# Attention with two mixture layers on one core: weight halves issued by ScalarE, a new order in the numerators, other banks for one slot sum

## Chip, cores and metric

One core of one Trainium2 chip runs the whole program. The metric is device time in microseconds, the median of three runs of the kernel.

## What is computed

A linear attention (features `exp(proj)` and `exp(-proj)`) feeds a soft mixture of 8 experts through 32 slots, and that feeds a second, dense mixture of 8 experts. Cut to what matters:

```python
# q, k, v: 4 batches x 8 heads x 576 x 64; w_phi 64 x 128
def phi(x):
    proj = einsum('bhsd,df->bhsf', x, w_phi)
    proj = proj - max(abs(proj), axis=-1, keepdims=True)
    return concatenate([exp(proj), exp(-proj)], axis=-1)
q_p, k_p = phi(q), phi(k)
kv  = einsum('bhsf,bhsd->bhfd', k_p, v);  z = sum(k_p, axis=2)
num = einsum('bhsf,bhfd->bhsd', q_p, kv)
den = einsum('bhsf,bhf->bhs', q_p, z) + 1e-06
x   = num / den                                   # 2304 tokens x 512

logits = x @ phi                                  # first mixture: 8 experts, 4 slots each
d = softmax of logits over the tokens;  slot_input = d.T @ x
slot_out[e] = relu(slot_input[e] @ w1[e]) @ w2[e] # w1 512 x 1024, w2 1024 x 512
x = softmax of logits over the slots @ slot_out

# second mixture: gates P by 8 rounds of row and column normalising, then for each expert
out += P[:, e] * (relu(x @ w1[e]) @ w2[e])
```

## The kernel before

The 2304 tokens are 18 tiles of 128. One hand-ordered loop, `for i in range(NT + LAG + 1)` (L414), carries the attention. Iteration `i` works on key tile `i` and, seven iterations late (`LAG = 7`), on query tile `t = i - 7`. So iterations 0 to 6 do keys alone, 7 to 16 do keys and queries, and from 17 on (`alone(i)`, L203) no new key tile is projected; those are called lone iterations here. All engines but GpSimd issue in the order in which the program is written (class `InOrder`, L43, with helper line L51, which is why nearly all rows of the trace carry L51).

What an iteration does, in order. SyncE issues the load of key tile `i + 3`, of a value block for tile `i + 2`, and of query tile `t + 3`, 256 KB each. TensorE projects the next query tile (`pq`, 32 matmuls) and the next key tile (`pk`), turns the finished rows of tile `t - 1` (`xt`), and turns query tile `t` in two halves (`ut`, `q_transpose(t, 0)` and `q_transpose(t, 1)`). ScalarE takes from each `ut` tile two exponentials (`phiq`, first of plus, then of minus). TensorE then does the logits (`lg`), adds the key tile into the sums (`kvacc`, 64 matmuls), and `q_num` multiplies the two query halves with the finished sums (`num`, 32 matmuls each). ScalarE takes four exponentials for the next key tile (`phik`) ahead of the numerators. In `q_num` the loop over the 4 heads is outside and the loop over the two signs `c` is inside it.

PSUM has named banks for this. `halves(t, hh)` (L206) gives banks A and E in the iterations with keys and E and C in lone ones, and both the `ut` tile and the `num` tile of a half are taken from that same bank: `num` can be written when both exponentials have read `ut`. Query projections use A and B.

Between the iterations a generator, `slot_inputs(g)` (L273), advances for each group of four tiles: a maximum, its broadcast, exponentials `dd`, and then the sums `pcs` (with ones) and `psi` (with the x tiles), which VectorE adds into `cs` and `si`. In group 1 `psi` lies in bank B and `pcs` in C, in groups 2 to 4 in A and B. Group 1's sums fall into the first lone iteration, number 17.

The weights of the first mixture come in 32 units of 1 MB, `units[u]`, each [128, 2048]; 22 of them are loaded during the attention. Units 0 to 3 (pool `wa`) and 8 to 14 (`early`, `wb`) are loaded in iterations 9 to 19 (`early_units`, L395) as two halves of 512 KB by `load_half` (L81), which issues on SyncE's queue: the first half between the key load and the value load, the second after the query load. Units 15 to 21 follow in iterations 18 to 24, both halves at the iteration's end (L487), in pool `wk`, which is opened where the key tiles lay, in iteration 18. Unit 4 waits for the last `pq` (its memory held the query tiles), units 5 to 7 for the end of the last numerators. After the loop the slots' experts run from about 193 us (`ph`, `po`), and then the second mixture, which is by far the longest stage.

Of the kernel before, what the change touches and what calls it, by code (L numbers as in the profile page):

```python
# [14 lines left out]
B, H, S, D = 4, 8, 576, 64  # L15
F = 128
NTOK, DM = B * S, H * D
NT = NTOK // 128
# [36 lines left out]
def tile_kernel(ctx: ExitStack, tc: tile.TileContext, a):  # L55
    nc = tc.nc
    PE, V, A, G, SP = nc.tensor, nc.vector, nc.scalar, nc.gpsimd, nc.sync

    const = ctx.enter_context(tc.tile_pool(name="const", bufs=1, side="left"))
    wa = ctx.enter_context(tc.tile_pool(name="wa", bufs=4, side="left"))  # L60
    early_cm = tc.tile_pool(name="early", bufs=1, side="left")
    early = early_cm.__enter__()
# [11 lines left out]
    unit_t = {}  # L74
# [6 lines left out]
    def load_half(pool, u, h):  # L81
        name, e, n = units[u]
        if h == 0:
            unit_t[units[u]] = pool.tile([128, 2048], F32, tag="w", name=f"{name}_{e}_{n}")
        r = slice(h * 1024, (h + 1) * 1024)
        SP.dma_start(out=unit_t[units[u]][:, r], in_=a[name][e, :, n * 2048:(n + 1) * 2048][:, r])

    def w1_unit(name, e, n):
        return unit_t[name, e, n].rearrange("p (k f) -> p k f", k=2)
# [16 lines left out]
    def mm(name, bank=None):  # L106
        if bank is None:
            bank = "ABCDE"[turn_of[0] % 5]
            turn_of[0] += 1
        return pmm.tile([128, 512], F32, tag=bank, name=name)  # L110
# [53 lines left out]
    def k_exp(t):  # L164
        us = uk_t.pop(t)
        phik = kp.tile([128, H, 2, F], F32, tag="phik", name=f"phik{t}")
        for j in range(2):
            for c in range(2):
                A.activation(out=phik[:, j::2, c, :], in_=h4(us[j]), func=AF.Exp, scale=1.0 if c == 0 else -1.0)
        phik_t[t] = phik  # L170
# [32 lines left out]
    def alone(i):  # L203
        return i + 1 >= NT
# [4 lines left out]
    def q_transpose(t, hh):  # L209
        ps = mm(f"ut{t}_{hh}", halves(t, hh))  # L210
        for j in range(4):
            PE.transpose(ps[:, j * 128:(j + 1) * 128], uq_t[t][hh][:, j * 128:(j + 1) * 128], ident)
        phiq = qp.tile([128, 2, 512], F32, tag="phiq", name=f"phiq{t}_{hh}", bufs=3)
        for c in range(2):
            A.activation(out=phiq[:, c], in_=ps, func=AF.Exp, scale=1.0 if c == 0 else -1.0)
        phiq_t[t, hh] = phiq
        if hh:
            uq_t.pop(t)
# [7 lines left out]
    def q_num(t, hh):  # L226
        if hh == 0:
            x_t[t] = (const if (t + 2) % XR < 6 else qp).tile([128, DM], F32, tag=f"x{(t + 2) % XR}", name=f"x{t}", bufs=1)
        phiq = phiq_t.pop((t, hh))
        ps = mm(f"num{t}_{hh}", halves(t, hh))  # L230
        for j in range(4):
            for c in range(2):
                for g in range(2):
                    b = (128 * t + 64 * g) // S
                    PE.matmul(
                        ps[g * 64:(g + 1) * 64, j * XW:(j + 1) * XW],
                        phiq[:, c, j * 128 + g * 64:j * 128 + (g + 1) * 64],
                        kvs_t[b][:, hh, j, c, :],
                        start=c == 0, stop=c == 1,
                    )  # L240
        pv = ps[:, 0:4 * XW].rearrange("p (h w) -> p h w", h=4)
        rd = qp.tile([128, 4, 1], F32, tag="rd", name=f"rd{t}_{hh}", bufs=2)
        V.tensor_scalar_add(rd, pv[:, :, XW - 1:XW], 1e-6)
        V.reciprocal(out=rd, in_=rd)
        V.tensor_tensor(
            out=x_t[t].rearrange("p (h d) -> p h d", h=H)[:, hh::2, :],
            in0=pv[:, :, 0:D], in1=rd.to_broadcast([128, 4, D]), op=ALU.mult,
        )
# [24 lines left out]
    def slot_inputs(g):  # L273

        ts, n = groups[g], len(groups[g])
        lgg = lg[:, ts[0]:ts[0] + n, :]
        gm4 = first.tile([128, 4, NS], F32, tag="gd", name=f"gm4{g}", bufs=1)
        if len(ts) == 2:
            V.tensor_tensor(out=gm4, in0=lgg[:, 0:1, :].to_broadcast([128, 4, NS]), in1=lgg[:, 1:2, :].to_broadcast([128, 4, NS]), op=ALU.max)
        else:  # L280
            gm = first.tile([128, 1, NS], F32, tag="gm", name=f"gm{g}", bufs=1)
            V.tensor_reduce(out=gm.rearrange("p o j -> p (o j)"), in_=lgg.rearrange("p t j -> p j t"), axis=AX.X, op=ALU.max)
            G.tensor_copy(out=gm4, in_=gm.to_broadcast([128, 4, NS]))
        yield
        last = g == len(groups) - 1
        pt = mm(f"gmt{g}", "B" if g > 1 else "C")
        keep_busy(last, 5)
        PE.transpose(pt[:, 0:128], gm4.rearrange("p g j -> p (g j)"), ident)
        mx = first.tile([128, 1], F32, tag="mx", name=f"mx{g}", bufs=2)
        V.tensor_reduce(out=mx, in_=pt[:, 0:128], axis=AX.X, op=ALU.max)  # L290
        if g:
            V.tensor_tensor(out=mx, in0=mx, in1=run["m"], op=ALU.max)
        dg = first.tile([NS, NS], F32, tag="gd", name=f"dg{g}", bufs=1)
        V.tensor_scalar_mul(dg, ident[0:NS, 0:NS], mx[0:NS])
        if g:
            al = first.tile([128, 1], F32, tag="al", name=f"al{g}", bufs=2)
            V.tensor_tensor(out=al, in0=run["m"], in1=mx, op=ALU.subtract)
            A.activation(out=al, in_=al, func=AF.Exp)
        run["m"] = mx
        yield  # L300
        pm = mm(f"gmb{g}", "B" if g > 1 else "C")
        keep_busy(last, 6)
        PE.matmul(pm[:, 0:NS], ones[0:NS, :], dg, start=True, stop=True)
        dd = first.tile([128, 4, NS], F32, tag="gd", name=f"dd{g}", bufs=1)
        V.tensor_tensor(out=dd[:, 0:n], in0=lgg, in1=pm[:, 0:NS].unsqueeze(1).to_broadcast([128, n, NS]), op=ALU.subtract)
        A.activation(out=dd[:, 0:n], in_=dd[:, 0:n], func=AF.Exp)
        if last:

            V.tensor_scalar_mul(sels[32 * n:128], sels[32 * n:128], al[32 * n:128])
        yield  # L310
        ps, pc = mm(f"psi{g}", "A" if g > 1 else "B"), mm(f"pcs{g}", "B" if g > 1 else "C")
        keep_busy(last, 4)
        for i in range(n):
            PE.matmul(pc[32 * i:32 * i + 32, 0:2], dd[:, i], ones[:, 0:2], start=True, stop=True)
        for i in range(n):
            PE.matmul(ps[32 * i:32 * i + 32, :], dd[:, i], x_t.pop(ts[i]), start=True, stop=True)
        r = slice(0, 32 * n)
        if g == 0:
            V.memset(si, 0.0)
            V.memset(cs, 0.0)  # L320
            V.tensor_copy(out=cs[r], in_=pc[r, 0:2])
            V.tensor_copy(out=si[r], in_=ps[r])
        else:
            V.scalar_tensor_tensor(out=cs[r], in0=cs[r], scalar=al[r], in1=pc[r, 0:2], op0=ALU.mult, op1=ALU.add)
            if last:

                csel = first.tile([128, NS], F32, name="csel")
                V.tensor_scalar_mul(csel, sels, cs[:, 0:1])
                pc = mm("pcsum", "D")
                PE.matmul(pc[:, 0:NS], ones, csel, start=True, stop=True)  # L330
            V.scalar_tensor_tensor(out=si[r], in0=si[r], scalar=al[r], in1=ps[r], op0=ALU.mult, op1=ALU.add)
            if last:
                V.tensor_scalar_add(rc.rearrange("p o j -> p (o j)"), pc[:, 0:NS], 1e-9)
                V.reciprocal(out=rc, in_=rc)
        if g < 3:
            yield
            slot_norm(g, 0)
            yield
            slot_norm(g, 1)
        yield  # L340
# [51 lines left out]
        for u in units[first:first + n]:  # L392
            load_unit(pool, *u)

    early_units = {9 + n: (wa, n) for n in range(4)}  # L395
    early_units |= {13 + n: (wb if n else early, 8 + n) for n in range(7)}
    si_steps = []

    def si_step():
# [14 lines left out]
    for i in range(NT + LAG + 1):  # L414
        t = i - LAG
        if i + 3 < NT:
            load_k(i + 3)
        if i in early_units:
            load_half(*early_units[i], 0)
        for n in [n for n, (u, _) in enumerate(VBLOCKS) if u == i + 2]:  # L420
            load_v(n)
        if 0 <= t + 3 < NT:
            load_q(t + 3)
        if i in early_units:
            load_half(*early_units[i], 1)
        if i == 1:
            SP.dma_start(out=sel4, in_=a["sel4"])
            SP.dma_start(out=wg, in_=a["wg"])
# [14 lines left out]
            x_turn(t - 1)  # L443
        if 0 <= t < NT:
            q_transpose(t, 0)
            q_transpose(t, 1)
        if 0 <= t - 1 < NT:
            if alone(i):
# [8 lines left out]
            k_project(i + 1)  # L457
        if i + 1 < NT:
            k_exp(i + 1)
        if not alone(i):  # L460
            si_step()
        if 0 <= t < NT:
# [17 lines left out]
            if n == len(groups[g]) - 1:  # L480
                si_steps.append(slot_inputs(g))
        si_step()
        if i == NT:
            kstack.close()
            wk_cm = tc.tile_pool(name="wk", bufs=7, side="right", reuse_waits="tile")
            wk = wk_cm.__enter__()
        if NT <= i < NT + 7:  # L487
            load_half(wk, 15 + i - NT, 0)
            load_half(wk, 15 + i - NT, 1)
    G = InOrder(tc, G)  # L490
    const.tile([128, 8], F32, name="pad", bufs=1)
    while si_steps:
# [549 lines left out]
```

## Time and profile before

| what | value |
|---|---|
| median of three runs | 1026.72 us (1024.71 to 1028.42) |
| the profiled execution | 1025.93 us |
| its span | 1024.2 us |
| granted TensorE clock, mean | 0.994 |
| TensorE matmul busy | 999.1 us, 98% |
| attention loop | until about 187 us |

The span is what the trace covers; some 1.7 us of the execution's own time lie around it. In the timeline a row gives the start, the time from the first start to the last end, engine, operation, tiles and count, and in brackets the idle time of the engine ahead of it with what ended it. "issue" stands for idle time for which the trace shows no releaser. A window gives each engine's busy time with its instruction count, then the granted clock, the busy share of the 16 DMA engines and what they moved.

### The profile page before, as it was taken

How to read it: one execution, taken by the hardware profiler on the slowest of the kernel's cores; microseconds unless marked ns; L12 is line 12 of the kernel's file. 1: busy time of each engine (PE TensorE's matmuls, PEld its weight loads, DVE VectorE, ACT ScalarE, POOL GpSimd, SP SyncE). 2: the span in 40 equal slices, each digit the busy share in tenths (PEclk: the TensorE clock that was granted, in tenths of full speed). 3: DMA queues.
4: the chain of work that ended last, by engine and by line, in shares of the span. 5: the costliest groups of instructions: out<-in, count | busy, mean ns of one | idle time of the engine just before them, and what ended most of it. 6: DMA issues, size and time to landing. Idle time of an engine off the chain costs nothing.

```text
span 1024.2 us, 27905 instructions
## 1 busy us (share of the span) xinstructions
PE 999.1 (98%) x11645; PEld 942.6 (92%) x11645; DVE 691.8 (68%) x1408; ACT 551.3 (54%) x993; POOL 594.8 (58%) x444
## 2 busy tenths in 40 slices
PE   8999899999999999999999999999999999999998
PEld 7888787538999999999999999999999999999998
DVE  5877777405788667677666676776666767767665
ACT  5564544226566666564555555555645555455452
POOL 1101000075578757777686778587857876777543
PEclk9999999999999999999999999999999999999999
DMA  6656672994000400130021003100300040000111
GB/s 205 217 155 201 211 248 83 355 409 190 1 1 2 165 2 1 49 118 1 2 97 70 2 1 124 43 2 1 130 36 2 1 165 2 1 1 24 61 43 62
DMA packets 25437, 89.23 MB, mean 87 GB/s; under 512 B 3424, under 2 KB 6240, under 8 KB 19424
## 3 DMA queue, kind: packets, MB, share of 16 engines
q1 hardware_dynamic: 25024, 86.93, 24.2%
q8 instruction: 92, 1.51, 0.6%
q0 software_dynamic: 288, 0.52, 0.2%
q14 instruction: 33, 0.27, 0.1%
HBM read 82.72 MB, written 4.72 MB: 85 GB/s over the span
## 4 chain that ended last, share of the span: by engine, by line
PE 92%; DVE 2%; DMA 2%; issue 1%; ACT 1%; POOL 0%; SPq 0%; DVEq 0%; ACTq 0%; POOLq 0%
PE x L51 38%; PE y L51 19%; PE z L51 16%; PE num L51 4%; PE kvacc L51 3%; DMA moe_w<-in_moe_w 2%; PE pq L51 2%; PE ut L51 2%; PE pk L51 2%; PE ps L51 1%; PE lg L51 1%; PE ph L51 1%; PE po L51 1%; ACT phiq L51 1%; PE xt L51 1%
## 5 line engine op out<-in xcount | busy, mean ns | idle before, releaser
L51 POOL TENSOR_TENSOR hl_s<-s,hh_s 128x512 fp32r<-128x512 f32 x287 | 366.3, 1298 | 212.1 <-ACT hh_s L51 190.5
L51 PE MATMUL x<-w_t,hh_s 128*128 128x256 f32 x1152 | 204.8, 278 | 0.0
L51 ACT ACTIVATE hh_s<-s 128x512 fp32r<-128x512 f32 x288 | 175.6, 630 | 52.1 <-DVE s L51 49.2
L51 ACT ACTIVATE r<-z 128x512 f32<-128x512 f32 x144 | 86.2, 598 | 165.6 <-PE z L51 164.8
L51 PEld LDWEIGHTS x<-w_t,hh_s 128*128 128x128 f32 x1152 | 173.5, 188 | 0.8
L51 DVE SCALAR_TENSOR_TENSOR xo<-x,P,xo 128x256 f32<-128x256 f32 x252 | 120.5, 478 | 69.9 <-PE x L51 69.9
L51 ACT ACTIVATE hh_a<-z 128x512 fp32r<-128x512 f32 x216 | 122.2, 600 | 75.8 <-DVE s L51 74.7
L51 PE MATMUL x<-w_t,hl_s 128*128 128x256 f32 x576 | 159.6, 277 | 0.0
L51 DVE SCALAR_TENSOR_TENSOR s<-z,r 128x512 f32<-128x512 f32 x144 | 98.6, 685 | 87.6 <-ACT hh_a L51 82.6
L51 DVE SCALAR_TENSOR_TENSOR hl_a<-z,hh_a 128x512 fp32r<-128x512 f32 x216 | 146.7, 679 | 0.0
L51 PEld LDWEIGHTS x<-w_t,hl_s 128*128 128x128 f32 x576 | 108.2, 188 | 0.0
L51 PE MATMUL y<-w_t,hh_s 128*128 128x256 f32 x576 | 102.9, 278 | 0.0
L51 PE MATMUL z<-w_b,hh_a 128*128 128x256 f32 x576 | 102.4, 278 | 0.0
L51 PE MATMUL x<-w_b,hh_a 128*128 128x256 f32 x576 | 102.0, 278 | 0.0
L51 PE MATMUL x<-w_t,hh_a 128*128 128x256 f32 x576 | 101.6, 276 | 0.0
L51 PE MATMUL y<-w_b,hh_s 128*128 128x256 f32 x576 | 101.5, 276 | 0.0
L51 DVE SCALAR_TENSOR_TENSOR s<-z,s 128x512 f32<-128x512 f32 x144 | 98.2, 682 | 3.7 <-POOL hl_s L51 1.4
L51 PEld LDWEIGHTS z<-w_b,hh_a 128*128 128x128 f32 x576 | 86.6, 188 | 2.9 <-issue 2.9
L51 PEld LDWEIGHTS y<-w_t,hh_s 128*128 128x128 f32 x576 | 87.4, 188 | 0.0
L51 PEld LDWEIGHTS x<-w_b,hh_a 128*128 128x128 f32 x576 | 87.2, 189 | 0.1
L51 PEld LDWEIGHTS x<-w_t,hh_a 128*128 128x128 f32 x576 | 86.7, 188 | 0.1
L51 PEld LDWEIGHTS y<-w_b,hh_s 128*128 128x128 f32 x576 | 86.7, 188 | 0.0
(167 smaller groups left out, 1991.2 us busy)
## 6 DMA issues: line engine op xcount, KB each, us to landing
moe_w<-in_moe_w SPq DMA_DIRECT2D x46, 1024.0 KB, 6.5
moe_w<-in_moe_w SPq DMA_DIRECT2D x36, 512.0 KB, 6.3
vs<-in_vb SPq DMA_DIRECT2D x20, 256.0 KB, 2.8
kt<-in_kT SPq DMA_DIRECT2D x18, 256.0 KB, 3.7
qt<-in_qT SPq DMA_DIRECT2D x18, 256.0 KB, 3.1
out<-xo SPq DMA_DIRECT2D x18, 128.0 KB, 1.7
out<-xo SPq DMA_DIRECT2D x9, 256.0 KB, 2.0
rep<-in_rep POOLq DMA_DIRECT2D x2, 256.0 KB, 3.4
```

Source lines behind the costliest of these rows:

```text
L51: return lambda *args, **kwargs: self.tc.keep_in_program_order(make(*args, **kwargs))
```

## The change

`load_half` issues on ScalarE's queue. Its calls move: in iterations 7 to 17 the halves of units 0 to 3 and 8 to 14, in 18 to 24 those of units 15 to 21. The first half is issued between the two `q_transpose` calls, that is between the exponentials of the two query halves, the second after the next key tile's exponentials. SyncE's queue no longer holds them. Pool `wk` is opened at the end of iteration 17 instead of 18. In `q_num` the loop over the sign `c` is outside and that over the heads inside, with one `start` for each half of the partitions. In group 1 `psi` moves to bank A and `pcs` to bank B.

```diff
     def load_half(pool, u, h):
-        SP.dma_start(out=unit_t[units[u]][:, r], in_=a[name][e, :, n * 2048:(n + 1) * 2048][:, r])
+        A.dma_start(out=unit_t[units[u]][:, r], in_=a[name][e, :, n * 2048:(n + 1) * 2048][:, r])
...
-        for j in range(4):
-            for c in range(2):
+        for c in range(2):
+            for j in range(4):
                 for g in range(2):
...
-                        start=c == 0, stop=c == 1,
+                        start=c == 0 and j == 0, stop=c == 1, skip_group_check=True,
...
-        ps, pc = mm(f"psi{g}", "A" if g > 1 else "B"), mm(f"pcs{g}", "B" if g > 1 else "C")
+        ps, pc = mm(f"psi{g}", "A" if g else "B"), mm(f"pcs{g}", "B" if g else "C")
...
-    early_units = {9 + n: (wa, n) for n in range(4)}
-    early_units |= {13 + n: (wb if n else early, 8 + n) for n in range(7)}
+    attn_units = {7 + n: (wa, n) for n in range(4)}
+    attn_units |= {11 + n: (wb if n else early, 8 + n) for n in range(7)}
...
-        if i in early_units:
-            load_half(*early_units[i], 0)
...
-        if i in early_units:
-            load_half(*early_units[i], 1)
...
             q_transpose(t, 0)
+            if i in attn_units:
+                load_half(*attn_units[i], 0)
             q_transpose(t, 1)
...
             k_exp(i + 1)
+        if i in attn_units:
+            load_half(*attn_units[i], 1)
...
-        if i == NT:
+        if i + 1 == NT:
             kstack.close()
...
-        if NT <= i < NT + 7:
-            load_half(wk, 15 + i - NT, 0)
-            load_half(wk, 15 + i - NT, 1)
+            attn_units |= {i + 1 + n: (wk, 15 + n) for n in range(7)}
```

## Rows read from the trace of the kernel before

**Rows 1.** The page: TensorE's instructions, and one of the DMA queues (packets, MB, share).
```profile
PE 999.1 (98%) x11645; PEld 942.6 (92%) x11645; DVE 691.8 (68%) x1408; ACT 551.3 (54%) x993; POOL 594.8 (58%) x444
...
q8 instruction: 92, 1.51, 0.6%
```
**Rows 2.** Waits of TensorE, 20 to 192 us: total us, times, longest us.
```profile
PE num L51 <- ACT phiq L51: 1.6, 5, 0.4
...
PE pcs L51 <- DVE x L51: 1.0, 1, 1.0
```
**Rows 3.** The chain that ended last, pieces in order: start us, us, what.
```profile
41.69 0.86 issue
...
52.13 1.10 issue
...
77.80 0.68 issue
...
94.24 0.71 issue
...
108.91 2.74 issue
```
**Rows 4.** Windows from the start to the first and the last of those places.
```profile
0.00:42.00 42.00, 37.08 (x977) 33.10 (x977) 29.09 (x46) 23.97 (x42) 7.75 (x28) 1.00 0.69 212
...
0.00:110.00 110.00, 99.87 (x2622) 88.08 (x2623) 80.42 (x159) 62.24 (x122) 14.31 (x49) 1.00 0.64 202
```
**Rows 5.** Windows before and behind the longest of them.
```profile
102.00:109.00 7.00, 6.77 (x178) 5.84 (x168) 6.34 (x14) 4.92 (x10) 0.67 (x2) 1.00 0.91 291
...
112.00:115.00 3.00, 3.00 (x64) 2.88 (x64) 1.25 (x4) 0.00 (x0) 0.00 (x0) 0.54 0.13 49
```
**Rows 6.** Timeline of SyncE's issues of weight halves.
```profile
55.93 1.53 SPq L51 DMA_DIRECT2D moe_w<-in_moe_w  x1
...
87.60 0.43 SPq L51 DMA_DIRECT2D moe_w<-in_moe_w  x1
...
102.55 1.66 SPq L51 DMA_DIRECT2D moe_w<-in_moe_w  x2
...
104.73 1.43 SPq L51 DMA_DIRECT2D moe_w<-in_moe_w  x2
```
**Rows 7.** Timeline of TensorE: a dense stretch, and two projections, slow and quick.
```profile
66.30 2.06 PE L51 MATMUL kvacc<-vt,phik 128*64 128x65 f32 x64
68.20 2.04 PE L51 MATMUL num<-kvs,phiq 128*64 128x65 f32 x64
...
112.50 1.98 PE L51 MATMUL pq<-wbd,qt 64*64 64x128 f32 x32
...
121.94 1.10 PE L51 MATMUL pq<-wbd,qt 64*64 64x128 f32 x32
```
**Rows 8.** Timeline of TensorE around the slot sums of groups 1 and 2.
```profile
135.36 2.04 PE L51 MATMUL num<-kvs,phiq 128*64 128x65 f32 x64
...
140.33 1.42 PE L51 MATMUL pq<-wbd,qt 64*64 64x128 f32 x32
...
163.47 2.13 PE L51 MATMUL num<-kvs,phiq 128*64 128x65 f32 x64
...
167.54 1.10 PE L51 MATMUL pq<-wbd,qt 64*64 64x128 f32 x32 [0.28 <-DVE si L51]
```
**Rows 9.** Timeline: exponentials with keys (65 us) and alone, and lone numerators.
```profile
65.25 2.06 ACT L51 ACTIVATE phiq<-ut 128x512 f32<-128x512 f32 x4
...
174.63 2.07 ACT L51 ACTIVATE phiq<-ut 128x512 f32<-128x512 f32 x4 [1.42 <-PE ut L51]
...
175.77 2.13 PE L51 MATMUL num<-kvs,phiq 128*64 128x65 f32 x64 [0.30 <-ACT phiq L51]
```
**Rows 10.** The chain in the slots' experts, and a window of that stage.
```profile
214.69 14.27 DMA moe_w<-in_moe_w
...
200.00:225.00 25.00, 24.74 (x306) 10.50 (x302) 3.13 (x18) 6.64 (x12) 14.81 (x11) 1.00 1.01 405
```

## Prediction

> **What bounds the kernel now.** I read the page first: TensorE's matmuls are busy 98% of the span [rows 1], so a change that takes no TensorE work away can win only where TensorE stands idle or runs slowly. The second mixture offers nothing of that kind and isn't touched. I therefore read TensorE's waits in the attention, then the chain that ended last in that stretch, then windows and timelines around each gap.
>
> In the attention the chain runs through TensorE nearly all the time. What it loses has three forms. The largest are five gaps that the chain calls issue, of 0.86, 1.10, 0.68, 0.71 and 2.74 us, 6.1 us together [rows 3]: nothing that the trace shows released TensorE. The second is one wait of 1.0 us of `pcs` for VectorE's `x`. The third is five short waits of `num` for the exponentials, 1.6 us in all [rows 2].
>
> What are the five gaps? The page lists 92 packets of 1.51 MB on an instruction queue, 16.4 KB each, and TensorE executes 11,645 matmuls and as many weight loads, so one packet is worth 253 of them [rows 1]. Up to the first gap the windows count 977 + 977 = 1954 of these, up to the last 2622 + 2623 = 5245: the difference, 3291, is 13.0 times 253 [rows 4]; the three between fall on multiples too. So TensorE stops where one block of its instructions ends and the next hasn't come. A block is eaten in as little as 3.9 us: `kvacc` and `num` with 64 matmuls each, 256 instructions with their weight loads, from 66.30 to 70.24 [rows 7]. The block has to arrive through the same 16 DMA engines as the weights. Ahead of the longest gap these were 91% busy over 7 us [rows 5], with four halves issued from 102.55 to 106.16 [rows 6]; at the 405 GB/s of a saturated stretch [rows 10] 512 KB are 1.3 us, so these four alone are 5.2 us. That gap also brought the granted clock to 0.54 over the next 3 us [rows 5], near the lower of its two levels, 1.2 GHz; the query projection took 1.98 us there and 1.10 us at full clock [rows 7], 0.9 us lost.
>
> The Trainium skill (Runtime: NRT & Kernel Launch, Instruction fetch mechanics) states blocks of 16 KiB, 256 instructions, and says that crossing from one to the next is mostly hidden. The first agrees with the 16.4 KB; the second does not hold at the five places if my reading of the counts is right. By that rule the gaps are something else, and nothing says that they go: that is the second case below.
>
> **The change, part by part.**
>
> *Weight halves spread out.* Bytes and transfers stay the same, 36 halves; their times change. On SyncE's queue halves run up behind a value load that waits for its buffer and are then let go together. After the change one comes between the two pairs of exponentials, in the middle of 65.25 to 67.31 in one iteration [rows 9], and one after the key exponentials behind them; each is 1.3 us of transfer, SyncE's three loads of 256 KB are 0.65 us each by the same rate. Even if all of an iteration's came together, that would be 2 x 1.3 + 3 x 0.65 = 4.6 us; four halves with loads between them, as from 102.55, can't meet any more. A block that comes at a good moment waits for nothing; one that comes right behind such a run still waits. Bounds: none of the five gaps left, 6.1 us won, or the same sum at other places, 0 won. I take three left at the mean of the four short ones, 0.84 us, so 2.5 us remain and 3.6 us are won. The long gap being the one made by the burst, the clock's 0.9 us go with it (bounds 0 and 0.9).
>
> In lone iterations the halves of units 15 to 19 now move later, into a stretch where the chain shows no such gap after 108.91 [rows 3]. Some four blocks are fetched there. Bounds: 0 and 4 x 0.84 = 3.4 us lost; I take 0.5, near the lower end, since lone iterations carry few other loads.
>
> *ScalarE's cost of issuing.* No row shows a transfer issued on ScalarE. The nearest are SyncE's: 0.43 us usually, 1.53 us at most for one half [rows 6]. With keys there is cover: the second query half's exponentials end at 67.31 and the second half of `num` starts in the middle of its 2.04 us, at 69.22 [rows 7, 9], 1.9 us later, so even 1.53 us are hidden; uncovered they would cost up to 11 times that. In lone iterations the cover is thin. The four exponentials run from 174.63 to 176.70, `num` starts at 175.77, its second half 1.07 us later at 176.84 [rows 9]: 0.14 us of slack. If an issue of 0.43 us delays the second pair in full, each of 7 lone iterations loses 0.29 us, 2.0 us together. But ScalarE was idle for 1.42 us ahead of the four exponentials [rows 9]; an issue that its sequencer does while the engine waits, or while it works on the pair before (1.0 us), costs nothing. Bounds 0 and 2.0; I take 0. A wait of the transfer for memory isn't to be feared: the pools are fresh up to unit 14, and the key tiles' memory is long free when lone iterations begin.
>
> *SyncE.* Its key, value and query loads no longer queue behind halves. They are issued two or three tiles ahead and no wait of TensorE in rows 2 or 3 is for them: 0.
>
> *Numerators.* The new order would let the first 16 matmuls of a half start after one exponential. But `num` takes the bank from which both exponentials read, so its first write waits for the second exponential as before. The gaps of 0.30 us [rows 9] stay: 0. Bound on the other side, if the wait were finer: the 1.6 us of all five waits [rows 2]. The number of matmuls and weight loads is the same.
>
> *Group 1's banks.* Before, `num` of the first lone iteration ended at 137.40 and the next projection began at 140.33, 2.93 us later. Between them lies the 1.0 us in which `pcs`, in bank C, waits until VectorE has read the numerators there [rows 2, 8]. Group 2, already in A and B, goes from 165.60 to 167.54, 1.94 us, a new wait of 0.28 us of the projection for `si` included, since bank A is now the projection's [rows 8]. So 2.93 - 1.94 = 1.0 us is won; what is late next is that 0.28 us.
>
> *Does the gain reach the end?* The slots' experts are bound by transfers: the chain has 14.27 us of weights in one piece, with the DMA engines at 1.01 of their time [rows 10]. A faster attention would be lost there if these loads had their own clock. They don't: unit 4 waits for the last projection and units 5 to 7 for the last numerators, so the whole stage starts earlier. Units 20 and 21, 2 MB, are issued in both versions around those two moments. I count 0, with 1.3 us (one half) as the worst.
>
> Sum: -3.6 - 0.9 + 0.5 + 0 + 0 + 0 - 1.0 = -5.0 us against the profiled execution, 1025.93 (its span is 1024.2): 1020.9. The median of the runs shown is 0.8 us above that execution, so I predict 1021.7.
>
> **Rivals.**
>
> *The gaps only move.* Every block border stays at the same instruction, and other borders may now meet a half. If the same 7.0 us (gaps and clock) are lost elsewhere, only the 1.0 us of the banks is won: 1025.7. For it: DMA engines still move the same bytes in the same stretch. Against: the 2.74 us needed a burst that can't form any more.
>
> *More fetches collide* (slower). Today halves and loads stand in one queue; then they stand in two. The mechanism: a block's packet takes turns with two busy queues. Place: the block borders of the iterations with keys and queries, 13 from 42 to 110 us alone [rows 4]. If ten instead of five stall at the present mean of 1.22 us, and the clock falls twice instead of once, 6.1 + 0.9 are added and 1.0 is won: 1026.7 + 6.0 = 1032.7. It decides as soon as more than about six borders stall for that long. The Trainium skill (DMA: Bandwidth & Descriptors, Queues, rings and completion order) says that an engine takes turns between the queues that have work, a packet at a time, which speaks for this rival; no row here has two queues full at once.
>
> *ScalarE's issue is exposed.* With the 2.0 us above, the forecast becomes 1023.7; at 1.53 us an issue it would be 1.39 x 7 = 9.7 us and about 1031. Against it speak the idle 1.42 us.
>
> *The change doesn't do what it says.* For the numerators I expect just that, by the bank.
>
> **How the numbers follow.** The forecast's own case, stalls reduced, 0.60: from 1017.5 (all gaps gone and clock kept: 1026.7 - 6.1 - 0.9 - 1.0 = 1018.7, and part of the 1.6 us of the numerators) to 1023.6. Gaps moved or the ScalarE cost partly exposed, 0.30: 1023.6 to 1029. Slower by more than that, 0.10: 1030 to 1033. A measurement of this kernel can tell about 0.3%, 3.1 us, from no change. So faster 0.60, same 0.30, slower 0.10. For 8 in 10 the range takes the first case and most of the second: 1017.5 to 1027.5.
>
> **What would show it.** Right: no issue gap over 1.2 us in the chain of the attention, at most three around 0.8 us, the clock at 1.00 throughout 22 to 130 us, the first lone projection 1.9 us behind its numerators, and 0.30 us of `num` waiting for `phiq` unchanged. Wrong: a gap of 2 us or more at another multiple of 253 instructions, or `num` in lone iterations waiting 0.5 us or more for `phiq`. If `num` starts before its second exponential ends, I was wrong on the banks. The prediction as a whole is wrong if the loads of the slots' experts start no earlier although the attention ends earlier.

## The result and the profile after

The changed kernel takes 1016.94 us (median of four runs, 1015.75 to 1018.05). The kernel before took 1027.41 us beside it (four runs, 1024.71 to 1028.42): a ratio of 0.9895 with a 95% interval of 0.9864 to 0.9926. By the ratio that is 10.8 us less, 7.6 to 14.0; the two medians lie 10.5 us apart. I had predicted 1021.7 us and a range down to 1017.5. The direction was right, the size was not: more was won than even the range allowed.

The profiled execution after the change took 1018.05 us, the longest of the four, with a span of 1016.3 us. Its waits of TensorE, 20 to 192 us (total us, times, longest us), stand against [rows 2]:

```profile
PE gmb L51 <- DVE al L51: 1.7, 3, 0.8
PE num L51 <- ACT phiq L51: 1.6, 5, 0.4
...
PE num L51 <- issue: 0.6, 1, 0.6
PE pq L51 <- DVE si L51: 0.6, 2, 0.3
```

The exponentials hold up `num` for 1.6 us in five waits, just as before. The wait of `pcs` for `x` is gone, and `pq` waits 0.3 us for `si` twice instead of once. The issue gaps of `num` are down from 5.4 us to 0.6 us, in one place. The chain of the attention and of the slots' experts after the change (start us, us, what) says the same of the gaps, against [rows 3], and gives the long transfer that answers to [rows 10]:

```profile
41.37 0.59 issue
...
205.88 15.39 DMA moe_w<-in_moe_w
```

One gap of 0.59 us is left of five with 6.09 us. (Both chains have one more short piece of 0.26 us at 24 us; its count of 1048 instructions is no multiple of a block away from the others, and it doesn't change.) Windows of the changed kernel show where it stands and what the place of the former long gap looks like now (columns as in [rows 4]):

```profile
0.00:41.60 41.60, 36.77 (x977) 32.81 (x977) 29.01 (x46) 23.97 (x42) 7.74 (x28) 1.00 0.72 214
...
98.50:105.50 7.00, 6.87 (x189) 6.06 (x180) 6.05 (x13) 4.83 (x10) 0.40 (x2) 1.00 0.62 194
...
105.00:108.00 3.00, 3.00 (x102) 2.77 (x98) 2.16 (x8) 0.59 (x2) 1.00 (x3) 1.00 0.58 188
```

The gap is at 977 + 977 instructions, the same count as the first gap before [rows 4]. The stretch that answers to [rows 5] has its DMA engines 62% busy instead of 91%, and the clock stays at 1.00 instead of 0.54.

How do the halves go out? ScalarE's timeline in one iteration after the change (start us, time from the first start to the last end), against [rows 9] and [rows 6]:

```profile
63.80 0.60 ACT L51 ACTIVATE phiq<-ut 128x512 f32<-128x512 f32 x1
63.81 0.34 ACTq L51 DMA_DIRECT2D moe_w<-in_moe_w  x1
64.30 1.57 ACT L51 ACTIVATE phiq<-ut 128x512 f32<-128x512 f32 x3
...
65.79 1.97 ACT L51 ACTIVATE phik<-uk 128x512 f32<-128x512 f32 x3
67.14 0.33 ACTq L51 DMA_DIRECT2D moe_w<-in_moe_w  x1
67.67 0.62 ACT L51 ACTIVATE phik<-uk 128x512 f32<-128x512 f32 x1
```

Of the 36 issues 34 take 0.33 or 0.34 us, the longest 0.74 us. The two here lie wholly beneath an exponential that is running: the issue at 63.81 us stands in the program behind two exponentials, of which the second starts only at 64.30 us. ScalarE's sequencer thus runs ahead by one exponential here, not further: the two halves of a unit go out 3.3 us apart, because the exponentials between them wait for TensorE's work. In lone iterations, where no key exponentials stand between them, they go out 0.8 to 1.8 us apart.

Where did the time come from? The same piece of work in TensorE's timeline of both kernels tells it. Rows after:

```profile
106.23 1.10 PE L51 MATMUL pq<-wbd,qt 64*64 64x128 f32 x32
...
114.63 1.41 PE L51 MATMUL pq<-wbd,qt 64*64 64x128 f32 x30
...
128.43 2.04 PE L51 MATMUL num<-kvs,phiq 128*64 128x65 f32 x64
...
132.40 1.10 PE L51 MATMUL pq<-wbd,qt 64*64 64x128 f32 x32 [0.28 <-DVE si L51]
...
154.42 2.39 PE L51 MATMUL num<-kvs,phiq 128*64 128x65 f32 x64
...
158.73 1.10 PE L51 MATMUL pq<-wbd,qt 64*64 64x128 f32 x32 [0.28 <-DVE si L51]
```

| work | before, from | after | earlier by | step |
|---|---|---|---|---|
| `pq` behind the long gap | 112.50 [rows 7] | 106.23 | 6.27 | gaps 5.5; the rest small stalls and slow clock |
| next `pq` | 121.94 [rows 7] | 114.63 | 7.31 | 1.0 more: clock |
| `num`, first lone iteration | 135.36 [rows 8] | 128.43 | 6.93 | 0.4 lost |
| next `pq` | 140.33 [rows 8] | 132.40 | 7.93 | 1.0: banks of group 1 |
| `num` ahead of group 2's sums | 163.47 [rows 8] | 154.42 | 9.05 | 1.1: lone iterations |
| next `pq` | 167.54 [rows 8] | 158.73 | 8.81 | 0.2 lost |
| start of the long transfer | 214.69 [rows 10] | 205.88 | 8.81 | 0 |
| its end | 228.96 | 221.27 | 7.69 | 1.1 lost |
| end of the span | 1024.2 | 1016.3 | 7.9 | 0.2 won |

### The profile page after: what moved, and what is told of

Same layout as the page of the kernel before. It is cut to its first block, busy times and chain, and to the rows that moved or that the text cites. A ratio compares the mean times of both kernels' runs of the same rounds, so it can differ in the third digit from the quotient of the medians.

```text
span 1016.3 us, 27901 instructions
## 1 busy us (share of the span) xinstructions
PE 996.7 (98%) x11645; PEld 940.4 (93%) x11645; DVE 691.7 (68%) x1408; ACT 551.6 (54%) x993; POOL 594.6 (59%) x444
## 4 chain that ended last, share of the span: by engine, by line
PE 94%; DVE 2%; DMA 2%; ACT 1%; issue 1%; SPq 0%; DVEq 0%; ACTq 0%
PE x L51 39%; PE y L51 19%; PE z L51 16%; PE num L51 4%; PE kvacc L51 3%; PE ut L51 2%; PE pq L51 2%; PE pk L51 2%; DMA moe_w<-in_moe_w 2%; PE ps L51 1%; PE lg L51 1%; PE ph L51 1%; PE po L51 1%; PE xt L51 1%; PE psi L51 0%
```

## Experiments

**Each part alone.** Three kernels: the kernel before with the banks alone, the kernel before with the numerators' order alone, and the change with only the halves moved.

```diff
 e1_banks, from the kernel before
-        ps, pc = mm(f"psi{g}", "A" if g > 1 else "B"), mm(f"pcs{g}", "B" if g > 1 else "C")
+        ps, pc = mm(f"psi{g}", "A" if g else "B"), mm(f"pcs{g}", "B" if g else "C")
 e2_order, from the kernel before
-        for j in range(4):
-            for c in range(2):
+        for c in range(2):
+            for j in range(4):
 e3_halves, from the changed kernel: both of these as in the kernel before
```

> The kernel before with group 1's slot sums in banks A and B, nothing else. My theory of the banks: the wait of pcs for x (1.0 us) goes, the projection behind it starts about 1.9 us after the numerators instead of 2.9, and 1.0 us is won in all; the five issue gaps stay, 6 us in sum, at the same instructions. Rival: the banks hold more of the 10 us than I gave them, 3 us or more.

> The kernel before with the sign outside the heads in the numerators, nothing else. My theory: the first write of num waits for both exponentials of its bank, so nothing moves: 0 us, and five waits of num for phiq of 0.3 to 0.4 us as before. Rival: num starts behind the first exponential, the 0.30 us gaps go and up to 1.6 us are won.

> The changed kernel with the numerators' order and group 1's banks as before, so only the weight halves on ScalarE's queue at their new places. My theory: nearly all of the gain is here, 9 us against the kernel before and 1.0 us less than the changed kernel; issue gaps of less than 1 us in sum between 30 and 130 us. Rival (several small parts that only together give it): half of the gain or less, 5 us.

Measured against 1026.14 us of the kernel before: the banks 1023.80 us, ratio 0.9986 (0.9965 to 1.0006), by the ratio 1.4 us less with an interval from 3.6 less to 0.6 more; the order 1025.49 us, ratio 1.0013 (0.9992 to 1.0034); the halves 1018.32 us, ratio 0.9925 (0.9901 to 0.9949), 7.7 us less. So the halves carry the change, the order alone does nothing, and the banks are worth about the 1.0 us of the trace, which the runs by themselves can't tell from none. For the halves alone I had expected gaps of less than 1 us in sum; their chain has 0.59 and 0.83 us. In the chain with the banks alone the gaps are still there:

```profile
77.64 1.50 issue
...
109.81 2.56 issue
```

In TensorE's waits with the order alone (first fence) `num` waits for the exponentials as long as ever, 1.6 us in [rows 2]. In those with the halves alone (second fence) the wait of `pcs` is back:

```profile
PE num L51 <- ACT phiq L51: 1.9, 6, 0.4
```
```profile
PE pcs L51 <- DVE x L51: 1.0, 1, 1.0
```

**Another queue, or another moment?** The changed kernel with the halves issued by SyncE, at the same places of the program.

```diff
-        A.dma_start(out=unit_t[units[u]][:, r], in_=...)
+        SP.dma_start(out=unit_t[units[u]][:, r], in_=...)
```

> The changed kernel with its halves issued by SyncE at the same places of the program, nothing else changed. Theory that the moment of issue does it: SyncE runs ahead of the others until a value load stops it, so halves are again let go together; issue gaps of 3 us or more in sum come back and the time is 1020 to 1025. Rival (the place in the program is what counts, whichever queue): 1017, as the changed kernel.

It took 1030.50 us, ratio 1.0044 (1.0024 to 1.0065): 4.5 us slower than the kernel before and some 13 slower than the change, with one word different. That is worse than the 1025 us at which my expectation ended. SyncE's timeline, two windows and TensorE's timeline of this kernel, in three fences:

```profile
107.53 0.90 SPq L51 DMA_DIRECT2D moe_w<-in_moe_w  x2
108.53 0.38 SPq L51 DMA_DIRECT2D qt<-in_qT  x1
108.95 2.22 SPq L51 DMA_DIRECT2D moe_w<-in_moe_w  x2
```
```profile
105.00:113.00 8.00, 7.86 (x218) 7.00 (x216) 5.97 (x13) 5.07 (x11) 1.08 (x4) 1.00 0.90 293
0.00:113.20 113.20, 99.90 (x2622) 87.89 (x2623) 80.05 (x159) 62.35 (x122) 13.81 (x48) 1.00 0.65 206
```
```profile
115.77 0.57 PE L51 MATMUL num<-kvs,phiq 128*64 128x65 f32 x13 [2.46 <-issue]
```

SyncE has no computation that holds it back. It runs to the next load that waits for a buffer, and once that is free the halves of two iterations and a query load go out within 3.6 us, one behind the other. The DMA engines are 90% busy and TensorE stops for 2.46 us at 2622 + 2623 instructions, exactly the count of the long gap before [rows 4], in `num` with 13 matmuls to go. A place in the program is not a moment: on ScalarE it is one, since the exponentials around it wait for data.

**How long may a run of transfers be?** On ScalarE again, now both halves of a unit together (1 MB), and, in iterations 7 to 16, two units together every second iteration (2 MB). Bytes, engine and queue are those of the change.

```diff
 e5_whole
             if i in attn_units:
                 load_half(*attn_units[i], 0)
+                load_half(*attn_units[i], 1)
 e6_pairs
-                load_half(*attn_units[i], 0)
+                if i < NT - 1:
+                    for n in (i, i + 1) if i % 2 else ():
+                        for h in range(2):
+                            load_half(*attn_units[n], h)
 both: the second place is dropped (e6_pairs: up to iteration 16)
```

> The changed kernel, with both halves of a unit issued by ScalarE one right behind the other, between the exponentials of the two query halves: runs of 1 MB, 2.6 us at 405 GB/s, instead of two runs of 512 KB. If what counts is that a weight transfer is short against the time in which a block of TensorE's instructions has to arrive (spacing), one or two more borders stall for 0.8 us: 1018 to 1019.5 us, with one or two issue gaps in TensorE's chain between 40 and 120 us. If what counts is only that the weights left SyncE's queue, nothing changes: 1017 us and the one gap of 0.6 us. If ScalarE's issue costs time by standing between exponentials, two issues (0.7 us) in that place show as num waiting for phiq in the lone iterations, 7 times 0.3 us: 1019 us, without issue gaps.

> The changed kernel, but in iterations 7 to 16 the four halves of two units are issued by ScalarE at once in every second iteration: five runs of 2 MB, 5.2 us at 405 GB/s. Bytes, engine and queue are as in the changed kernel. Spacing theory: a border of instruction blocks that falls into one of these runs stalls as before the change; 38% of some 13 borders are about 5, half of them badly: 1019.5 to 1023 us, with at least one issue gap over 1 us between 50 and 120 us. Queue theory (it is enough that weights don't stand in SyncE's queue): 1017 us, no gap over 0.6 us. Cost of the issue: four issues of 0.34 us in one place hold up the second query half's exponentials by up to 1.0 us; with keys num has 1.9 us of slack, so 0.

Against 1027.40 us of the kernel before: runs of 1 MB 1022.34 us, ratio 0.9954 (0.9935 to 0.9973); runs of 2 MB 1022.75 us, ratio 0.9958 (0.9941 to 0.9974). Half of the gain is given back by either. The queue theory falls: both use ScalarE's queue. Gaps from the chain of e5_whole (first fence) and of e6_pairs (second); ahead of them both have the one at 42 us:

```profile
52.48 1.45 issue
...
63.69 1.41 issue
...
119.48 0.81 issue
```
```profile
48.57 1.34 issue
...
65.03 1.02 issue
...
86.79 1.13 issue
```

I had expected one or two gaps of 0.8 us for 1 MB and got 1018 to 1019.5 us wrong by three: a run of 2.6 us already makes gaps of 1.4 us, and twice that length makes them no longer. So in the iterations with keys 512 KB with other work between nearly pass unnoticed, and 1 MB doesn't. Lone iterations are another matter: there the changed kernel lets two halves go within 0.8 to 1.8 us, and its chain shows no such gap. A small part of the loss of e5_whole is not a gap of this kind: in the lone iteration at 151 us the two issues in a row hold up the exponentials behind them, and `num` waits 0.62 us for `phiq`.

**Is it really the border of a block?** The windows of e6_pairs up to its last four gaps count 2205, 2965, 3977 and 5751 instructions, that is 1954 (its first gap) plus 251, 4 x 253, 8 x 253 and 15 x 253. The counter-test adds 64 instructions to the warm-up of the kernel before, so that every border falls into other work.

```diff
 e7_shift, from the kernel before
-    for j in range(6):
+    for j in range(3):
         PE.matmul(pt[:, j % 4 * 128:j % 4 * 128 + 128], still, still, start=True, stop=True)
+    for j in range(19):
+        PE.matmul(pt[:, 0:1], still, still[:, 0:1], start=True, stop=True)
```

> The kernel before, with 64 more TensorE instructions (matmuls and weight loads) in the warm-up, made of fewer large and more small matmuls so that the work behind it starts at nearly the same time. Nothing else is changed. Block theory: the issue gaps stand where a multiple of some 256 instructions since the start is reached, so each now falls 64 instructions earlier in the work: the count of matmuls and weight loads up to a gap leaves the same remainder as in the kernel before. Rival (a gap belongs to a place in the work, such as the wait for a value load): the count up to each gap is 64 more than before. The time may go either way by which loads a border now meets: 1022 to 1030 us by both.

Two gaps of its chain, windows up to them, and TensorE's timeline around the second, in three fences:

```profile
57.13 1.23 issue
...
115.09 2.01 issue
```
```profile
0.00:57.30 57.30, 52.57 (x1230) 48.08 (x1230) 35.85 (x60) 28.90 (x54) 8.44 (x30) 1.00 0.60 188
0.00:115.50 115.50, 106.51 (x2623) 94.86 (x2623) 79.61 (x156) 61.91 (x122) 13.40 (x47) 1.00 0.60 186
```
```profile
114.33 0.75 PE L51 MATMUL num<-kvs,phiq 128*64 128x65 f32 x20
117.10 1.50 PE L51 MATMUL num<-kvs,phiq 128*64 128x65 f32 x44 [2.01 <-issue]
```

The counts are 2460 and 5246: 1954 plus 2 and 13 times 253. With 64 instructions more ahead of it the gap at 5246 stands where it stood, at the 5245 of [rows 4], and cuts `num` after 20 matmuls instead of 51. That is 31 matmuls earlier; the 64 instructions are 32, with their weight loads. For these gaps the rival, a place in the work, is refuted. How a gap of the rival's kind behaves shows the short piece of 0.26 us: its count goes from 1048 to 1112, 64 more, and it stays in its place in the work. In the fourteen traces of this case the chains have 39 gaps of TensorE longer than 0.62 us up to 200 us, and each stands within 5 instructions of 1954 plus or minus a multiple of 253. The time says nothing here: 1037.49 us, outside my 1022 to 1030, but the warm-up itself now lasts 9.55 us instead of 2.93, since the small matmuls still load whole weights. That is 6.6 of the 10.1 us; the rest is more gaps, some 10 us instead of 6.

The changed kernel without the weight halves in the attention asks the opposite: which gap isn't theirs?

```diff
 e10_noload
-        A.dma_start(out=unit_t[units[u]][:, r], in_=...)
+        nc.gpsimd.memset(unit_t[units[u]][:, r], 0.0)
```

> The changed kernel without the 36 loads of weight halves in the attention: GpSimd fills those tiles with zeros, so the first mixture computes with zeros in place of 18 units of its weights. Everything else, the load of keys, values and queries and of the other units included, is as in the changed kernel. If TensorE's issue gaps come from instruction blocks that arrive late among weight transfers, no gap but the one at 41 to 42 us is left (in the kernel before it stands ahead of the first weight half, when keys, values and queries alone keep the DMA engines 69% busy), and TensorE reaches the end of the attention 0 to 0.6 us earlier than after the change. If gaps stay at other multiples of some 253 instructions, the loads of keys, values and queries make them too. The total says little, since the loads left out are missing in the DMA queues: 1012 to 1017 us.

Its chain up to 200 us has these two issue pieces (first fence) and the short one of 0.26 us; the second fence shows windows up to the later one, around it and behind it:

```profile
17.36 0.40 issue
45.71 0.86 issue
```
```profile
0.00:45.90 45.90, 38.53 (x977) 34.97 (x977) 28.98 (x46) 24.00 (x42) 27.16 (x50) 0.96 0.60 183
42.00:46.00 4.00, 3.71 (x101) 3.40 (x99) 3.34 (x6) 3.14 (x6) 0.66 (x2) 1.00 0.23 70
46.60:190.00 143.40, 136.88 (x3290) 116.47 (x3290) 110.17 (x267) 74.29 (x165) 24.11 (x48) 1.00 0.27 85
```

The gap at 977 + 977 stays without any half. I had written that in the kernel before it stands ahead of the first half; it doesn't, a first half is issued at 38.0 us there and at 38.1 us after the change. But it needs none. That keys, values and queries make it is not shown: the DMA engines are 23% busy in the 4 us around it, and why this block comes late stays open. Behind it there is none, over 6580 instructions or some 26 borders. The new piece at 17.36 and the later start come from GpSimd, whose zeros held up `vt` by 2.2 us, so the total (1018.49 us, above the 1012 to 1017 that I had expected) can't be used.

**Does ScalarE pay for the issues?** The changed kernel with twice as many, each of half the size.

```diff
 e8_quarters
+        for k in range(2):
-        r = slice(h * 1024, (h + 1) * 1024)
+            r = slice(h * 1024 + k * 512, h * 1024 + (k + 1) * 512)
             A.dma_start(out=unit_t[units[u]][:, r], in_=...)
```

> The changed kernel, with each half of 512 KB issued by ScalarE as two quarters of 256 KB, back to back: twice as many issues on ScalarE (36 more, 0.34 us each as the trace after the change shows them, 12 us in all), the same bytes at the same moments. If ScalarE's issues are hidden under the exponential that runs (as I now read it): within 1.5 us of the changed kernel, 1016 to 1018.5 us. If they cost ScalarE time that reaches TensorE, the lone iterations lose 0.3 us or more each, and num waits longer for phiq there: 1019 to 1021 us.

1018.55 us, ratio 0.9915 (0.9893 to 0.9938), at the edge of what the hidden issue allows. Its chain has gaps of 0.59, 0.83 and 0.61 us, 1.4 us more than the 0.59 us of the change in its profile; `num` waits 1.8 us for `phiq`, 0.2 us more. The 72 issues take longer than I had reckoned, 0.43 us in the middle and 1.44 us at most. Where a pair takes longer than the exponentials that cover it, ScalarE does stand idle:

```profile
126.38 1.81 ACTq L51 DMA_DIRECT2D moe_w<-in_moe_w  x2
...
128.30 1.08 ACT L51 ACTIVATE phiq<-ut 128x512 f32<-128x512 f32 x2 [0.88 <-ACT phiq L51]
```

`num` behind it, at 128.95 us, doesn't wait. So 36 more issues cost at most 1.6 us in the median, and the gaps account for nearly all of that.

**The numerators, and one more wait.** I had said that the order gains nothing because a numerator takes the bank from which its own exponentials read. Then it must gain with other banks. And one wait is the same before and after, that of group 2's `gmb`, 0.80 and 0.82 us.

```diff
 e11_numbank, from the changed kernel
-        ps = mm(f"num{t}_{hh}", halves(t, hh))
+        ps = mm(f"num{t}_{hh}", "AE"[hh] if alone(t + LAG) else halves(t, hh))
 e9_gmb, from the changed kernel: gmb of group 2 behind the next q_project, in bank D
-        pm = mm(f"gmb{g}", "B" if g > 1 else "C")
+        pm = mm(f"gmb{g}", "D" if g == 2 else "B" if g > 1 else "C")
 e12_both: both
```

> The changed kernel; in lone iterations the two numerators lie in banks A and E, not in E and C, the banks from which their own exponentials read. All instructions and their order are the same. My reading of the numerators (the new order of signs gains nothing because the bank is the wait): now it can, num starts after the first exponential, its five waits of 0.3 us for phiq in lone iterations go, 1.5 us in all: 1015.5 us. Rival (num waits for both exponentials for another reason, or the wait is hidden behind xt): the waits stay, 1017 us. If the next projection or ut then waits for VectorE's reading of the numerators, up to 7 times 0.3 us are lost: 1018 to 1019 us.

> The changed kernel, with one small step moved: gmb of group 2, for which TensorE waits 0.82 us at 149.05 us in the trace after the change, comes behind the next query projection and lies in bank D instead of B. That wait is the same in every trace of this case (0.80 to 0.82 us), and in the changed kernel the granted clock falls behind it to 0.78 and 0.65 for two stretches of 3 us. If the idle time is the only loss, 0.8 us are won: 1016.1 us. If the clock falls because of this idle time, it stays at 1.00 from 150 to 156 us and up to 1.3 us more are won in the executions that had it: 1015 us. If the wait only moves (pcs or the next ut waits instead), 1017 us.

> The changed kernel with both edits, gmb of group 2 moved and the lone numerators in banks A and E. If the two gains are separate, they add: 0.8 to 2.1 us and 1.5 us, 1013.5 to 1015 us. If the slots' experts behind, which are bound by transfers, take the gain back, the total stays above 1015.5 us although the attention ends 2 us earlier.

In TensorE's waits of e11_numbank, longest first, the 1.6 us of `num` for `phiq` would stand ahead of these lines; they are gone, and 0.6 us of `ut` for `x` have come:

```profile
PE pk L51 <- DVE uk L51: 1.0, 1, 1.0
PE ut L51 <- DVE x L51: 0.6, 1, 0.6
```

The time is 1015.63 us (1014.19 to 1015.92), the lowest of the study, ratio 0.9891 (0.9869 to 0.9913). The bank was the wait: shown by the waits. That it is also faster than the change as measured, 1016.94 us, is likely by its size, 1.3 us where 1.5 were expected, but the two ratios overlap. The next two kernels, which differ by these banks alone, lie 1.6 us apart in the same direction.

Moving `gmb` was a miss: 1019.19 us alone and 1017.61 us with the banks. TensorE no longer waits 0.82 us, but `xt`, next in bank D, waits longer for the same work. From TensorE's waits of e9_gmb:

```profile
PE xt L51 <- DVE dd L51: 1.5, 1, 1.5
```

VectorE works in order, and `dd` now stands behind four operations of the projection (0.69 us each). The granted clock of e9_gmb fell all the same, to 0.69 from 153 to 156 us. I had looked at TensorE's queue and not at VectorE's.

## Why the prediction was off

**The bound** was read rightly: gaps at block borders, while transfers run. The counts of the long gaps in all traces, above all in e7_shift, show it, and so does the time of the packets (last section). The Trainium skill (Runtime: NRT & Kernel Launch, Instruction fetch mechanics) calls crossings mostly hidden. With the DMA engines 27% busy (e10_noload) that holds for every border behind the first gap; behind a run of 1 MB or more in the iterations with keys it does not hold.

**Weight halves: the step that failed, in its size.** The sum had this term too small: I put three gaps of 0.84 us left and 3.6 us won; one of 0.59 us is left and 5.5 us are won. "Three left" was a middle between bounds and came from no row. The better step was at hand: a half is 1.3 us of transfer, and if the halves lie 3.3 us apart, as they do with keys, a border meets one half at most. The change against e5_whole and e6_pairs shows that a single one costs little and two in a row cost more. The first gap, at 41 us, needs no half (e10_noload), and it is the one that stays.

**The clock** was mis-sized in the same step: 0.9 us from one projection; the table gives 1.0 us between the two projections, and the end of `num` and the projection behind it ran slowly as well, about 1.4 us in all. **Lone iterations** I put at 0.5 us lost; 0.9 us are won there (1.1 less 0.2), and 0.4 us lost just ahead of them. The 1.1 us are 0.3 in the projection at 140.33 us (1.42 us [rows 8] against 1.10), 0.4 in `num` at 154.30 us, which has a border in it (2.55 us against 2.13), and 0.4 behind group 2's `gmb`, where the granted clock was 0.86 and 0.57 in two windows of 3 us before the change and 0.78 and 0.65 after it. I had priced what the moved halves might do there and not what the trace loses there without them.

**What I took to cost nothing cost nothing that shows.** ScalarE's issue lies under an exponential (the timeline), as long as it is a single one; pairs of issues did hold ScalarE up in places (e5_whole, e8_quarters). No wait for keys, values or queries came. The numerators gained nothing, and for the reason given (e2_order, e11_numbank). **Group 1's banks** gave the 1.0 us that the rows of group 2 promised, with the 0.28 us for `si` behind it.

**The slots' experts** took back 1.1 us in this execution, within the 1.3 us that I had set as the worst; I had taken 0. It is no toll on an earlier start: in e11_numbank the same piece begins 0.27 us earlier and ends 1.5 us earlier:

```profile
205.61 14.20 DMA moe_w<-in_moe_w
```

**The base.** The steps sum to 7.9 us between the two profiled spans, but the medians lie 10.5 us apart. The profiled execution after the change, 1018.05 us, lies inside my range, the median 0.6 us below its end. Part of that is the luck of four runs. The profile of before is 1.5 us below its median in this comparison, but over all 71 executions of the kernel before on record the median is 1026.23 us, 0.3 us above the profile; against it the change wins 9.3 us. The profile after is 1.1 us above its median. Both 7.9 and 9.3 us lie in the interval of 7.6 to 14.0. My range ended at 1017.5 because it began from one execution with one set of gaps. In the kernel before these vary, and so do the times: 1019.6 to 1031.8 us in the 71 executions, 1015.8 to 1018.1 us in the four of the changed kernel. That a change which takes away what varies gains more in the median than in one pair of profiles is my reading; it is not shown.

**Rivals.** "The gaps only move" gave 1025.7 us and didn't happen; e7_shift shows what moving looks like. "More fetches collide" gave 1032.7 us; e4_on_sync, at 1030.5 us, shows more borders stalled, but with one queue instead of two: what decides there is how many transfers are let go together. The rule on queues that I had cited from the Trainium skill (DMA: Bandwidth & Descriptors, Queues, rings and completion order) led me to fear the second queue; after the change two are in use, and fewer borders stall. The exposed issue on ScalarE didn't happen.

## What to carry to other kernels

Where a chain shows gaps that nothing released, count the engine's instructions up to each: if the counts differ by multiples of one block, suspect a late instruction block; here the gaps behind the first came with the weight transfers, and the longest where several were let go in a row. Issue such transfers one at a time from an engine whose queue is paced by the computation, not from one that runs ahead to its next buffer wait; the place in the program alone does not set the moment. Before an in-order engine's step is moved, look at what it will stand behind on every engine that it uses.

## What the runs showed of the hardware

ScalarE's sequencer issued 512 KB mostly in 0.33 or 0.34 us while an exponential ran, at no cost that the trace after the change shows. A block of instructions is delayed ahead of its packet, not in it. In the DMA view of the kernel before, from 108.0 to 109.2 us, where the long gap begins (first fence: queue, packets, MB, share of 16 engines), the data queue has its engines more than fully busy and no packet of instructions is seen; one comes in the next 1.1 us (second fence), with 5.2% of 16 engines' time, 0.92 us, and TensorE goes on at 111.65 us:

```profile
q1 hardware_dynamic: 167, 0.46, 102.8%
```
```profile
q1 hardware_dynamic: 144, 0.41, 96.3%
q8 instruction: 1, 0.02, 5.2%
```

The other gaps end in the same way. In the kernel before one packet of this queue comes between each two borders. Those ahead of the five gaps start at 40.09, 50.86, 76.06, 92.59 and 109.33 us, 2.6 to 4.4 us after TensorE passed the border before, and TensorE goes on 2.3 to 2.5 us after each start. Over the 14 borders behind the first gap the time from one border to the next packet has a median of 2.3 us before the change, 1.6 us after it and 0.6 us without the halves (e10_noload). This is the time that the spread halves shorten.

Open is the clock in lone iterations. TensorE waits 0.8 us ahead of group 2's `gmb` in the changed kernel (until 149.86 us) and in e3_halves (until 151.58 us). Behind it, in windows of 3 us, the granted clock is 0.78 and 0.65 in the one (first fence) and stays at 1.00 in the other (second fence). No run here tells what decides.

```profile
150.00:153.00 3.00, 2.99 (x40) 2.53 (x41) 1.66 (x4) 0.67 (x4) 0.00 (x0) 0.78 0.00 0
153.00:156.00 3.00, 3.00 (x50) 2.67 (x51) 1.39 (x4) 2.36 (x5) 0.00 (x0) 0.65 0.65 186
```
```profile
153.00:156.00 3.00, 2.70 (x54) 2.29 (x46) 2.61 (x4) 1.92 (x4) 0.00 (x0) 1.00 0.28 64
```
